# Dynamic convolution and a tanh-shrink MLP on one core: a tile in halves, a first x tile without halo, a longer accumulating DMA

## The chip, the cores and the metric

The kernel runs on one core of one Trainium2 chip. The metric is the device time of one execution in microseconds. Lower is better.

## The reference

Two steps in a row. `x` is (8, 4096, 192), `weight_gen` is (8, 4096, 8 heads, 7 taps), both f32.

```python
w = softmax(weight_gen, axis=-1)                    # 7 taps per token and head
x_pad = 6 zero rows ahead of each sequence
conv[b, s, h, g] = sum over k of w[b, s, h, k] * x_pad[b, s + k, h, g]     # 24 channels a head
h = conv.reshape(32768, 192) @ w_in                 # (192, 2048)
out = (h - tanh(h)) @ w_out                         # (2048, 192)
```

## The kernel before

**Tiling.** The 32768 tokens are cut into 32 blocks of 1024 (`NTOT`). Within a block each of the 128 partitions holds 8 neighbouring tokens (`J`), and its x tile holds 14 rows: 6 rows of halo ahead of the 8 (`HALO + J`). Partitions overlap in their halo, so that each of the 7 taps is a plain slice of the tile. The 192 channels are handled as three chunks of 64 (`NC`, `R`).

**Convolution.** `products` multiplies the x rows by the softmax weights, one instruction a tap, into bf16 tiles: `even` (taps 0, 2, 4), `odd` (taps 1, 3, 5) and `last` (tap 6). GpSimd (POOL) does nearly all of these; VectorE (DVE) does four taps of block 0 and two of block 1. From block 3 on, a DMA issued by POOL adds the first 4096 of the 4608 elements of `odd` to `even` in place (L201), so that fewer tiles have to be summed. `conv` then transposes and sums the tiles on TensorE (PE) against an identity, accumulating in PSUM: groups `even` 0 to 2, `last`, and for chunk 2 alone also the pair of `odd` that the DMA leaves out. ScalarE (ACT) copies the sum to `convT` (L244).

**MLP.** `gemm1` makes one of 16 f tiles: six matmuls into a PSUM tile `ph` of 1024 columns (L257), a tanh on ACT (L267), and a subtraction on DVE that reads the PSUM tile again and writes bf16 `gt` (L269). There are three PSUM buffers for `ph` and for the transposes' `pc`, taken in turn. `gemm2` sums one token block of the previous block's 16 `gt` tiles (L289), and ACT copies the result out (L307).

**Order.** The order of the instructions on each engine is written out by hand (`manual_schedule`). The main loop runs over blocks n; inside, eight steps p each do f tiles 2p and 2p+1 of block n and one `gemm2` of block n-1. The transposes of block n+1 come at p = 6, behind f tiles 12 and 13 and ahead of f tiles 14 and 15. The products of block n+2 are put on POOL at p = 0, so POOL works about two blocks ahead. A dependency (L177) holds their first instruction back until the last subtraction then issued.

**Start.** SyncE (SP) issues the loads of `weight_gen` and x: for block 0 the zero rows of the halo, row 0, partitions 1 to 15, partitions 16 to 127. POOL issues the load of `w_in` in two parts, f tiles 0 to 7 ahead of its products and 8 to 15 behind its products of block 0 (`FA`); each part is copied once more within SBUF, by a DMA issued from ACT and from SP (L369).

Of the kernel before, what the change touches and what calls it, by code (L numbers as in the profile page):

```python
# [11 lines left out]
ACT = mybir.ActivationFunctionType  # L12
# [4 lines left out]
def kernel(  # L17
# [8 lines left out]
    nc = tc.nc  # L26

    B, S, D = x.shape
    H, K = weight_gen.shape[2], weight_gen.shape[3]
    G = D // H  # L30
    F = moe_w_in.shape[1]
    P = nc.NUM_PARTITIONS
    R = P // 2
    HALO = K - 1

    J = 8
    TOK = P * J
# [3 lines left out]
    NTOT = B * NSB  # L41
    NFT = F // P
    NC = D // R
    GC = G // NC
    NPAIR = K // 2
    ACC = NPAIR * J * D - J * R
    PLAIN = (0, 1, 2)
    assert S % TOK == 0 and D % R == 0 and H * GC == R and F % P == 0
    assert NFT == 2 * J, "one token block of the second matmul per pair of f tiles"
# [23 lines left out]
    prods_of = {}  # L73
    conv_of = {}
    g_of = {}
    last_act = {}
    g1_act = {}
    last_sub = {}
    last_wsm = {}

    def order(inst, other, reason):
        tc.add_manual_dep(
            inst.ins,
            other.ins.name,
            mybir.DependencyInfo(mybir.DependencyClass.Sync, mybir.DependencyReason.DATA),
            reason=reason,
        )

    def load_wg(n):
        b, s = divmod(n, NSB)  # L90
        s0 = s * TOK
        wg_t = wgpool.tile([P, J, H, K], FP32, name="wg_t")
        nc.sync.dma_start(  # L93
            out=wg_t[:],
            in_=weight_gen[b, s0 : s0 + TOK].rearrange("(p j) h k -> p j h k", p=P),
        )
        wg_of[n] = wg_t

    def load_x(n):
        b, s = divmod(n, NSB)  # L100
        s0 = s * TOK

        x_t = xpool.tile([P, HALO + J, D], FP32, name="x_t")

        def rows(p0, p1):
            win = x[b, s0 + p0 * J - HALO : s0 + p0 * J - HALO + 1]
            nc.sync.dma_start(
                out=x_t[p0:p1, :, :],
                in_=bass.AP(
                    tensor=win.tensor,  # L110
                    offset=win.offset,
                    ap=[[J * D, p1 - p0], [D, HALO + J], [1, D]],
                ),
            )

        if s == 0:
            nc.sync.dma_start(  # L117
                out=x_t[0:1, 0:HALO, :],
                in_=zero[:].rearrange("o (h d) -> o h d", h=1).to_broadcast([1, HALO, D]),
            )  # L120
            nc.sync.dma_start(  # L121
                out=x_t[0:1, HALO : HALO + J, :],
                in_=x[b, 0:J].rearrange("(p j) d -> p j d", p=1),
            )

            rows(1, 16)
            rows(16, P)
        else:
            rows(0, P)
        x_of[n] = x_t  # L130
# [31 lines left out]
    def scale(eng, wsm, e_t, zr):  # L162
        return eng.tensor_mul(  # L163
            wsm.rearrange("p j h k -> p (j h) k"),
            e_t[:].rearrange("p j h k -> p (j h) k"),
            zr.rearrange("p (n o) -> p n o", o=1).to_broadcast([P, J * H, K]),
        )

    def products(n, on_vector=(), sums=None, hooks={}, behind=None):
        x_t = x_of.pop(n)  # L170
        wsm, wsm_v, e_t, zr = wsm_of.pop(n)
        if e_t is not None:
            first = scale(nc.gpsimd, wsm[:], e_t, zr[:])
            if behind is not None:


                order(first, behind, "pace")  # L177
        in_pairs = n not in PLAIN

        even = ppool.tile([P, NPAIR, NC, J, H, GC], BF16, name="even")  # L180
        odd = ppool.tile([P, NPAIR, NC, J, H, GC], BF16, name="odd")
        last = ppool.tile([P, NC, J, H, GC], BF16, name="last")
        dst = {}
        for i in range(NPAIR):
            dst[2 * i] = even[:, i]
            dst[2 * i + 1] = odd[:, i]
        dst[K - 1] = last[:]
        if -1 in hooks:
            hooks[-1]()
        for k in range(K):  # L190
            eng, w = (nc.vector, wsm_v) if k in on_vector else (nc.gpsimd, wsm[:])
            eng.tensor_mul(  # L192
                dst[k].rearrange("p c j h g -> p j h c g"),
                x_t[:, k : k + J, :].rearrange("p j (h c g) -> p j h c g", h=H, c=NC),
                w[:, :, :, k : k + 1]
                .rearrange("p j h (k o) -> p j h k o", o=1)
                .to_broadcast([P, J, H, NC, GC]),
            )
            if k == K - 2 and in_pairs:

                nc.gpsimd.dma_start(  # L201
                    out=even[:].rearrange("p i c j h g -> p (i c j h g)")[:, 0:ACC],
                    in_=odd[:].rearrange("p i c j h g -> p (i c j h g)")[:, 0:ACC],
                    accum_op=mybir.AluOpType.add,
                    max_dma_last_dim=4096,
                )
            if k in hooks:
                hooks[k]()
        if in_pairs:
            groups = [even[:, i] for i in range(NPAIR)] + [last[:]]  # L210
            prods_of[n] = [
                groups + ([odd[:, NPAIR - 1]] if c == NC - 1 else []) for c in range(NC)
            ]
        else:
            prods_of[n] = [[dst[k] for k in (sums or range(K))]] * NC

# [32 lines left out]
        if parts[-1][-1] == NC - 1:  # L249
            prods_of.pop(n)  # L250

    def gemm1(n, f):
        convT = conv_of[n]
        ph = psum_h.tile([P, 2, HT], FP32, name="ph", tag="ph")
        for c in range(NC):
            for r in range(2):
                nc.tensor.matmul(  # L257
                    ph[:, r, :],
                    lhsT=w_in[r * R : (r + 1) * R, c, f * P : (f + 1) * P],
                    rhs=convT[r * R : (r + 1) * R, c, :],  # L260
                    start=(c == 0),
                    stop=(c == NC - 1),
                )
        th = tpool.tile([P, TOK], FP32, name="th")
        ph_f = ph[:].rearrange("p r t -> p (r t)")
        g1_act[0] = last_act.get(0)
        last_act[0] = nc.scalar.activation(out=th[:], in_=ph_f, func=ACT.Tanh)  # L267
        gt = gpool.tile([P, TOK], BF16, name=f"gt{f}", tag=f"gt{f}")
        last_sub[0] = nc.vector.tensor_sub(gt[:], ph_f, th[:])  # L269
        g_of.setdefault(n, []).append(gt)  # L270

    LAST = (NTOT - 1) * J
# [76 lines left out]
    def load_w_out():  # L349
        nc.gpsimd.dma_start(out=w_out[:], in_=moe_w_out.rearrange("(c p) e -> p c e", c=NFT))  # L350

    FA = 8 * P

    def load_w_in(f0, f1):

        for c in range(NC):
            src = moe_w_in[c * GC : c * GC + 1, f0:f1]
            dma = nc.gpsimd.dma_start(
                out=w_in[0:R, c, f0:f1],
                in_=bass.AP(  # L360
                    tensor=src.tensor, offset=src.offset, ap=[[G * F, H], [F, GC], [1, f1 - f0]]
                ),
            )
            if f0 == 0:

                order(dma, last_wsm[0], "order of the loads")

    def copy_w_in(f0, f1, eng):
        eng.dma_start(out=w_in[R:P, :, f0:f1], in_=w_in[0:R, :, f0:f1])  # L369

    def rest_of_w_in():
        load_w_in(FA, F)

    load_wg(0)
    load_x(0)
    softmax_exp(0)
    softmax_norm(0, obank[0])
    load_wg(1)
    load_x(1)
    load_w_in(0, FA)  # L380
    products(
        0,
        on_vector=(3, 4, 5, 6),
        sums=(3, 0, 4, 5, 1, 6, 2),
        hooks={2: rest_of_w_in},
    )
    softmax_exp(1)
# [1 line left out]
    load_wg(2)  # L389
    copy_w_in(0, FA, nc.scalar)  # L390
    copy_w_in(FA, F, nc.sync)
    products(1, on_vector=(0, 1), hooks={4: load_w_out})
    conv(0, (0, 1), (2,))
    load_x(2)
    for n in range(NTOT):
        if n + 3 < NTOT:
            load_wg(n + 3)
            load_x(n + 3)
        for p in range(J):
            gemm1(n, 2 * p)  # L400
            gemm1(n, 2 * p + 1)
            if n == 0 and p == 1:
                softmax_exp(2)
            if p == 5 and n + 3 < NTOT:
                softmax_exp(n + 3)
            if n >= 1:
                gemm2((n - 1) * J + p)
            if p == 0 and 1 <= n < NTOT - 2:
                products(n + 2, behind=last_sub[0] if n > 1 else None)
            if n + 1 < NTOT:  # L410
                if p == (6 if n > 0 else 7):
                    conv(n + 1, (0, 1))
                if p == (6 if n > 1 else 7):
                    conv(n + 1, (2,))
            if n == 0 and p == 2:
                softmax_norm(2)
                products(2)
            if p == 6 and n + 3 < NTOT:
                softmax_norm(n + 3)
# [33 lines left out]
```

The softmax here doesn't subtract the row's maximum and nothing guards it: scores larger than these inputs give would overflow.

## Time and profile before

| What | Value |
|---|---|
| Median of 3 runs | 770.32 us (770.04 to 771.87) |
| The profiled execution | 770.86 us, span 768.7 us |
| PE, PEld busy | 736.7 us (96%), 583.1 us (76%) |
| DVE, ACT, POOL busy | 652.9 us, 640.8 us, 695.2 us |
| L269, subtraction, 512 times | 1219 ns each |
| L267, tanh, 512 times | 1022 ns each |
| L192 on POOL, one tap | 2903 ns each |
| L201, accumulating DMA, 29 times | 1202 ns to issue, 8.8 us to landing |

The profile is of one execution. PE is TensorE's matmuls and PEld its weight loads, which overlap. A line of the timeline has the start and the duration in microseconds, the engine, the line of the kernel, the operation, what it writes and reads, how many instructions are merged, and in brackets the idle time before it and what ended that. A line that gives three numbers behind a count has the shortest, median and longest duration in nanoseconds, and the first and last start.

### The profile page before, as it was taken

The page shows a single profiled execution, that of the slowest core. Times are in us where ns is not written, and L with a number is a line of the kernel's source. Part 1 is how long each engine was busy: PE and PEld are TensorE (multiplying, and loading weights), DVE is VectorE, ACT ScalarE, POOL GpSimd, SP SyncE. Part 2 cuts the span into 40 slices and gives each one's busy share as a digit, 9 for nine tenths or more (in the row PEclk, how much of TensorE's full clock was granted, in tenths as well). Part 3 has the DMA queues.
Part 4 walks back from the last instruction along what each step waited for, and adds up shares of the span by engine and source line. Part 5 has one row for each costly group of instructions (what it writes and reads, how often), then busy time and mean ns, then how long its engine had stood idle before and what let it go on. Part 6 is the DMA issues. An engine that isn't in the chain of part 4 may idle for free.

```text
span 768.7 us, 32330 instructions
## 1 busy us (share of the span) xinstructions
PE 736.7 (96%) x14784; PEld 583.1 (76%) x14784; DVE 652.9 (85%) x595; ACT 640.8 (83%) x865; POOL 695.2 (90%) x290
## 2 busy tenths in 40 slices
PE   2799999999999999999999999999999999999997
PEld 2377787777777777788777777777778777787777
DVE  5987888888898888889888888888888988888883
ACT  1777878888888888888888888888888888888883
POOL 5999999999999999999999999999999999999100
PEclk9999999999999999999999999999999999999999
DMA  7823776555677555577655557765556765542412
GB/s 209 184 81 87 182 181 150 118 145 147 169 182 174 131 129 148 150 180 182 164 123 133 150 160 182 180 128 137 143 150 172 182 181 115 125 142 72 98 43 84
DMA packets 25847, 111.37 MB, mean 145 GB/s; under 512 B 4800, under 2 KB 9456, under 8 KB 21624
## 3 DMA queue, kind: packets, MB, share of 16 engines
q1 hardware_dynamic: 14688, 76.95, 29.9%
q0 software_dynamic: 10816, 31.99, 25.8%
q8 instruction: 115, 1.88, 1.0%
q10 hardware_dynamic: 208, 0.39, 0.2%
q14 instruction: 20, 0.16, 0.1%
HBM read 54.49 MB, written 25.17 MB: 104 GB/s over the span
## 4 chain that ended last, share of the span: by engine, by line
PE 93%; DVE 2%; issue 1%; POOL 1%; DMA 1%; ACT 1%; SPq 0%; POOLq 0%
PE ph L257 43%; PE obank L289 43%; PE pc L233 6%; DVE gt L269 2%; PE po L323 1%; DMA x_t<-in_x_dram 1%; POOL even L192 1%; ACT th L267 0%; ACT convT L244 0%; POOL odd L192 0%; DVE zr L151 0%; DVE zsum L145 0%; SPq L117 0%; SPq L93 0%; SPq L121 0%
## 5 line engine op out<-in xcount | busy, mean ns | idle before, releaser
L269 DVE TENSOR_TENSOR gt<-ph,th 128x1024 bf16<-128x1024 f32 x512 | 602.8, 1219 | 93.3 <-ACT th L267 92.7
L267 ACT ACTIVATE th<-ph 128x1024 f32<-128x1024 f32 x512 | 497.2, 1022 | 65.7 <-PE ph L257 64.9
L257 PE MATMUL ph<-convT,w_in 64*128 64x512 bf16 x3072 | 382.1, 378 | 7.5 <-DVE gt L269 5.0
L289 PEld LDWEIGHTS <-gt 64*128 64x128 bf16 x7936 | 345.1, 94 | 53.4 <-issue 2.5
L289 PE MATMUL obank<-w_out,gt 64*128 64x192 bf16 x7936 | 374.6, 243 | 2.9 <-issue 2.1
L192 POOL TENSOR_TENSOR even<-x_t,wsm 128x1536 bf16<-128x1536 f32 x94 | 272.8, 2903 | 3.9 <-DMA x_t<-in_x_dram 1.6
L192 POOL TENSOR_TENSOR odd<-x_t,wsm 128x1536 bf16<-128x1536 f32 x93 | 269.9, 2903 | 0.0
L257 PEld LDWEIGHTS <-w_in 64*128 64x128 bf16 x3072 | 180.1, 94 | 108.4 <-issue 11.8
L192 POOL TENSOR_TENSOR last<-x_t,wsm 128x1536 bf16<-128x1536 f32 x31 | 103.4, 3336 | 0.0
L307 ACT ACTIVATE out_sb<-obank 128x192 f32<-128x192 f32 x248 | 81.9, 330 | 10.5 <-PE obank L289 4.6
L244 ACT ACTIVATE convT<-pc 128x1024 bf16<-128x1024 f32 x64 | 48.9, 808 | 31.6 <-PE pc L233 31.5
L233 PE MATMUL pc<-ident,even 64*128 64x64 bf16 x2304 | 47.9, 192 | 2.9 <-POOL even L192 1.5
L233 PEld LDWEIGHTS <-even 64*128 64x128 bf16 x2304 | 42.7, 96 | 4.1 <-issue 2.2
L201 POOL DMA_DIRECT2D even<-odd x29 | 34.9, 1205 | 9.1 <-POOL odd L192 9.1
L163 POOL TENSOR_TENSOR wsm<-e_t,zr 128x448 f32<-128x448 f32 x30 | 41.7, 1390 | 0.0
L233 PE MATMUL pc<-ident,odd 64*128 64x64 bf16 x448 | 15.5, 198 | 13.1 <-DVE odd L192 12.8
L135 ACT ACTIVATE e_t<-wg_t 128x448 f32<-128x448 f32 x32 | 18.5, 578 | 8.2 <-DMA wg_t<-in_weight_gen_dram 8.2
L233 PE MATMUL pc<-ident,last 64*128 64x64 bf16 x768 | 23.3, 192 | 1.8 <-issue 1.7
L145 DVE TENSOR_REDUCE zsum<-e_t 128x64 f32<-128x448 f32 x32 | 19.5, 609 | 2.9 <-ACT e_t L135 2.9
L233 PEld LDWEIGHTS <-odd 64*128 64x128 bf16 x448 | 11.3, 100 | 13.6 <-DVE odd L192 12.9
L151 DVE RECIPROCAL zr<-zsum 128x64 f32<-128x64 f32 x30 | 16.6, 553 | 3.0
L233 PEld LDWEIGHTS <-last 64*128 64x128 bf16 x768 | 17.0, 96 | 2.2 <-issue 1.8
(20 smaller groups left out, 48.7 us busy)
## 6 DMA issues: line engine op xcount, KB each, us to landing
x_t<-in_x_dram SPq DMA_DIRECT2D x24, 1344.0 KB
even<-odd POOLq DMA_DIRECT2D x29, 1024.0 KB, 8.8
out_dram<-out_sb SPq DMA_DIRECT2D x31, 768.0 KB
x_t<-in_x_dram SPq DMA_DIRECT2D x8, 1176.0 KB
wg_t<-in_weight_gen_dram SPq DMA_DIRECT2D x32, 224.0 KB
x_t<-in_x_dram SPq DMA_DIRECT2D x8, 157.5 KB
w_in<-in_moe_w_in_dram POOLq DMA_DIRECT2D x6, 128.0 KB, 7.5
w_out<-in_moe_w_out_dram POOLq DMA_DIRECT2D x1, 768.0 KB, 10.8
```

The source lines that it names most:

```text
L135: nc.scalar.activation(out=e_t[:].rearrange("p j h k -> p (j h k)"), in_=wg_t[:].rearrange("p j h k -> p (j h k)"), func=ACT.Exp,)
L145: nc.vector.reduce_sum(out=zsum[:], in_=e_t[:].rearrange("p j h k -> p (j h) k"), axis=AX.X)
L163: return eng.tensor_mul(wsm.rearrange("p j h k -> p (j h) k"), e_t[:].rearrange("p j h k -> p (j h) k"), zr.rearrange("p (n o) -> p n o", ...
L192: eng.tensor_mul(dst[k].rearrange("p c j h g -> p j h c g"), x_t[:, k : k + J, :].rearrange("p j (h c g) -> p j h c g", h=H, c=NC), w[:, : ...
L201: nc.gpsimd.dma_start(out=even[:].rearrange("p i c j h g -> p (i c j h g)")[:, 0:ACC], in_=odd[:].rearrange("p i c j h g -> p (i c j h g)" ...
L233: nc.tensor.matmul(pc[:, r, col : col + R], lhsT=prods[c][gi][r * R : (r + 1) * R, c, 2 * j : 2 * j + 2].rearrange("p j h g -> p (j h g)") ...
L244: nc.scalar.activation(out=convT[:, c0 : c0 + nch, :].rearrange("p c (j r t) -> p r (c j) t", r=2, t=R), in_=pc[:, :, 0 : nch * JH * R].re ...
L257: nc.tensor.matmul(ph[:, r, :], lhsT=w_in[r * R : (r + 1) * R, c, f * P : (f + 1) * P], rhs=convT[r * R : (r + 1) * R, c, :], start=(c == ...
L267: last_act[0] = nc.scalar.activation(out=th[:], in_=ph_f, func=ACT.Tanh)
L269: last_sub[0] = nc.vector.tensor_sub(gt[:], ph_f, th[:])
L289: mm = nc.tensor.matmul(po[:, 0:D], lhsT=g_of[n][f][r * R : (r + 1) * R, col : col + P], rhs=w_out[r * R : (r + 1) * R, f, :], start=(r == ...
L307: last_act[0] = nc.scalar.activation(out=out_sb[:, j, :], in_=po[:, 0:D], func=ACT.Copy)
```

## The change

Three edits. (1) In blocks 1 to 30, f tile 12, the one at p = 6, does its tanh and its subtraction in two halves of 512 columns. (2) The accumulating DMA covers all three pairs in full, 4608 elements a partition, given as three rows of 1536; the transposes of the last `odd` pair for chunk 2 go. (3) Block 0: x comes as 8 rows for all partitions first, then the halo of partitions 16 to 127, that of 1 to 15, and the zero rows last; the taps are taken in the order 6, 0, 3, 1, 4, 5, 2 and summed in the order 6, 3, 0, 4, 5, 1, 2; the first part of `w_in` has 7 f tiles instead of 8.

```diff
-    ACC = NPAIR * J * D - J * R
...
-        if s == 0:
-            nc.sync.dma_start(out=x_t[0:1, 0:HALO, :], in_=zero...)
-            nc.sync.dma_start(out=x_t[0:1, HALO : HALO + J, :], in_=x[b, 0:J]...)
-            rows(1, 16)
-            rows(16, P)
+        if n == 0:
+            rows(0, P, HALO, HALO + J)
+            rows(16, P, 0, HALO)
+            rows(1, 16, 0, HALO)
+            no_halo()
+        elif s == 0:
+            no_halo()
+            rows(0, 1, HALO, HALO + J)
             rows(1, 16)
             rows(16, P)
...
-        for k in range(K):
+        for k in order_of or range(K):
...
                 nc.gpsimd.dma_start(
-                    out=even[:].rearrange("p i c j h g -> p (i c j h g)")[:, 0:ACC],
-                    in_=odd[:].rearrange("p i c j h g -> p (i c j h g)")[:, 0:ACC],
+                    out=even[:].rearrange("p i c j h g -> p i (c j h g)"),
+                    in_=odd[:].rearrange("p i c j h g -> p i (c j h g)"),
                     accum_op=mybir.AluOpType.add,
                     max_dma_last_dim=4096,
                 )
...
-            groups = [even[:, i] for i in range(NPAIR)] + [last[:]]
-            prods_of[n] = [
-                groups + ([odd[:, NPAIR - 1]] if c == NC - 1 else []) for c in range(NC)
-            ]
+            prods_of[n] = [[even[:, i] for i in range(NPAIR)] + [last[:]]] * NC
...
-    def gemm1(n, f):
+    def gemm1(n, f, parts=1):
...
-        last_act[0] = nc.scalar.activation(out=th[:], in_=ph_f, func=ACT.Tanh)
-        last_sub[0] = nc.vector.tensor_sub(gt[:], ph_f, th[:])
+        for q in range(parts):
+            t0, t1 = q * TOK // parts, (q + 1) * TOK // parts
+            last_act[0] = nc.scalar.activation(
+                out=th[:, t0:t1], in_=ph_f[:, t0:t1], func=ACT.Tanh
+            )
+            last_sub[0] = nc.vector.tensor_sub(gt[:, t0:t1], ph_f[:, t0:t1], th[:, t0:t1])
...
-    FA = 8 * P
+    FA = 7 * P
...
-        on_vector=(3, 4, 5, 6),
-        sums=(3, 0, 4, 5, 1, 6, 2),
+        on_vector=(6, 3, 4, 5),
+        order_of=(6, 0, 3, 1, 4, 5, 2),
+        sums=(6, 3, 0, 4, 5, 1, 2),
...
-            gemm1(n, 2 * p)
+            gemm1(n, 2 * p, 2 if p == 6 and 0 < n < NTOT - 1 else 1)
```

More of the change, by code (lines that the diff above doesn't have):

```diff
@@ L103, in load_x, with rows @@
         x_t = xpool.tile([P, HALO + J, D], FP32, name="x_t")
-        def rows(p0, p1):
-            win = x[b, s0 + p0 * J - HALO : s0 + p0 * J - HALO + 1]
+        def rows(p0, p1, r0=0, r1=HALO + J):
+            win = x[b, s0 + p0 * J - HALO + r0 : s0 + p0 * J - HALO + r0 + 1]
             nc.sync.dma_start(
-                out=x_t[p0:p1, :, :],
+                out=x_t[p0:p1, r0:r1, :],
                 in_=bass.AP(
@@ L111, in rows, with no_halo @@
                     offset=win.offset,
-                    ap=[[J * D, p1 - p0], [D, HALO + J], [1, D]],
+                    ap=[[J * D, p1 - p0], [D, r1 - r0], [1, D]],
                 ),
             )
-        if s == 0:
+        def no_halo():
             nc.sync.dma_start(
@@ L120, in load_x @@
             )
[L121 to L124, printed above, removed]
+        if n == 0:
[6 more added lines that the diff above has]
+            rows(0, 1, HALO, HALO + J)
             rows(1, 16)
@@ L167, in scale, with products @@
         )
-    def products(n, on_vector=(), sums=None, hooks={}, behind=None):
+    def products(n, on_vector=(), order_of=None, sums=None, hooks={}, behind=None):
         x_t = x_of.pop(n)
@@ L360, in load_w_in @@
                 in_=bass.AP(
-                    tensor=src.tensor, offset=src.offset, ap=[[G * F, H], [F, GC], [1, f1 - f0]]
+                    tensor=src.tensor,
+                    offset=src.offset,
+                    ap=[[G * F, H], [F, GC], [1, f1 - f0]],
                 ),
```

## The prediction, made before the changed kernel was run

> **What bounds the kernel now.** I read the page's busy shares and chain first, then the timeline of one late block, then the issues on GpSimd, then the start.
>
> ```profile
> PE 736.7 (96%) x14784; PEld 583.1 (76%) x14784; DVE 652.9 (85%) x595; ACT 640.8 (83%) x865; POOL 695.2 (90%) x290
> ...
> PE 93%; DVE 2%; issue 1%; POOL 1%; DMA 1%; ACT 1%; SPq 0%; POOLq 0%
> ```
>
> TensorE carries the chain. POOL's 90% needs care: it is idle only at the two ends, so in between it is full too. The timeline around the transposes of block 25 (the other late blocks repeat it every 22.63 us):
>
> ```profile
> 589.56 1.94 ACT L267 ACTIVATE th<-ph 128x1024 f32<-128x1024 f32 x2
> ...
> 590.61 2.36 DVE L269 TENSOR_TENSOR gt<-ph,th 128x1024 bf16<-128x1024 f32 x2 [0.26 <-ACT th L267]
> ...
> 592.46 1.51 ACT L244 ACTIVATE convT<-pc 128x1024 bf16<-128x1024 f32 x2 [0.60 <-PE pc L233]
> ...
> 592.68 0.20 PEld L233 LDWEIGHTS <-odd 64*128 64x128 bf16 x8
> ...
> 592.80 1.20 PEld L257 LDWEIGHTS <-w_in 64*128 64x128 bf16 x12
> ...
> 593.02 1.47 PE L257 MATMUL ph<-convT,w_in 64*128 64x512 bf16 x12
> ...
> 593.88 1.94 ACT L267 ACTIVATE th<-ph 128x1024 f32<-128x1024 f32 x2
> ...
> 594.94 2.36 DVE L269 TENSOR_TENSOR gt<-ph,th 128x1024 bf16<-128x1024 f32 x2 [0.79 <-ACT th L267]
> ...
> 595.63 1.48 PE L257 MATMUL ph<-convT,w_in 64*128 64x512 bf16 x12
> ```
>
> The reader is to see a small stall that the page doesn't list. Tile 14's weights load at 592.80; in other pairs the matmul follows 0.08 later (588.61 and 588.69, 595.55 and 595.63). Here it starts at 593.02, 0.05 after the subtraction of tile 13 ends (590.61 + 2.36 = 592.97): three `ph` buffers, and tile 14 takes that of tile 13. So TensorE loses 592.88 to 593.02, 0.14 us a block. The eight `odd` transposes (592.68 to 592.80) lie ahead of this wait.
>
> ```profile
> 573.94 1.20 POOL L201 DMA_DIRECT2D even<-odd  x1 [0.30 <-POOL odd L192]
> 574.72 3.37 POOL L192 TENSOR_TENSOR last<-x_t,wsm 128x1536 bf16<-128x1536 f32 x1
> 577.59 1.42 POOL L163 TENSOR_TENSOR wsm<-e_t,zr 128x448 f32<-128x448 f32 x1
> ...
> 596.59 1.20 POOL L201 DMA_DIRECT2D even<-odd  x1 [0.30 <-POOL odd L192]
> ```
>
> POOL's own period is 596.59 - 573.94 = 22.65 us: as long as TensorE's, with no wait but that ahead of the DMA. What saves it is a lead. The last accumulating DMA is issued at 710.17, lands 8.8 us later in the median (11.1 at most), and its transposes start at 727.09; the first is issued at 75.77 for 88.47. Landing leaves about 4 us at the start, 6 to 8 later.
>
> **What the Trainium skill says.** "DMA: Bandwidth & Descriptors", Anatomy of one DMA, has many descriptors emitted before their incremental cost shows. The trace agrees:
>
> ```profile
> L201 POOL DMA_DIRECT2D even<-odd x29: 1202/1202/1244, 75.8 to 710.2; - x29
> L350 POOL DMA_DIRECT2D w_out<-in_moe_w_out_dram x1: 1233/1233/1233, 29.2 to 29.2; - x1
> L358 POOL DMA_DIRECT2D w_in<-in_moe_w_in_dram x6: 562/580/788, 6.8 to 20.0; - x6
> ```
>
> POOL's queue moves 2064 packets in the stretch of `w_out` and 272 in that of one accumulation, and both issues cost 1.2 us; `w_in` with 64 rows costs 0.58. The issue goes with rows (9.4 ns each), not pieces. The same page, SDMA does more than copy, caps an accumulating element at 2048 elements; 272 packets are 128 rows in two pieces of 2048 and 16 for the semaphore, so it agrees. Three pieces of 1536 a row then make 384. "GPSIMD Engine Reference", section 4, has a pair of cores write the descriptors; `last`, starting 0.78 after the DMA and taking 3.37 instead of 2.90, fits. "VectorE: DVE Perf Modes", the TRN2 errata, charges a fixed latency per instruction; here 192 elements take 357 ns, 1024 take 1219, 1536 take 1748: 1.036 ns an element and 158 ns fixed.
>
> **Part 1, the tile in halves (blocks 1 to 30).** One tanh and one subtraction become two each: 30 more on ACT, 30 more on DVE. ACT: 192 elements 330 ns, 1024 1022 ns, so 0.832 ns an element and 0.60 us for 512 (the 512-wide copy at L244 takes 0.60). Start to start, 1024 take 0.92 (1.94 - 1.02), so 512 take 0.92 - 0.43 = 0.49. DVE start to start: 1.14, so 512 take 0.61. In the block above, the first half's tanh ends at 590.16, tile 13's tanh starts at 589.56 + 2 x 0.49 = 590.55 instead of 590.48 and ends at 591.57. DVE is free at 590.28 (588.00 + 2 x 1.14), does the halves at 590.29 and 590.90, and tile 13 at 591.60 (0.03 after its tanh) instead of 591.755; it ends at 592.81. Tile 14 may start at 592.86, **0.16 earlier**. Behind the later tanh wait the `out_sb` copy (0.07 later, into ACT's 0.60 of idle) and the copies to `convT`, which wait for TensorE. Nothing there becomes late.
>
> What is late next: tile 14's tanh. ACT's `convT` copies start at 592.46, set by transposes that the change leaves alone, and occupy it to 593.38 + 0.48 = 593.86; the tanh gains 0.02 only. Its subtraction then ends at about 596.14, and the next block's second tile, which takes that buffer, can start at 596.19. It now starts at 595.63 + 0.65 (half of 594.31 - 593.02) = 596.28. **Gain: 0.09 us a block**. Below: 0, should another wait sit there; above: 0.16, should that one not bind. I take 0.09 x 29 = **2.6 us** (0 to 4.6).
>
> **Part 2, all 4608 elements.** Removes 8 matmuls and 8 loads a block, 15 ns each, 0.12 us; this lies ahead of the same wait, so alone it is worth nothing, and with part 1 TensorE is ready at 592.76, before the 592.86 of the gate. I count 0. It adds an eighth to the bytes and half to the pieces. Landing: by bytes 6.4 us of transfer (16 packets an engine of 0.4) become 7.2, so 9.6 us; by pieces 9.6, so 12 us. Both stay inside the 4 us. Packets of other queues have to share: PE's short gaps put to "issue" (5.7 us in all) could move either way by 1 us. The issue: 0 if rows count (taken), +0.41 us if a descriptor costs what lies between `w_in` (64: 0.58) and the accumulation (256: 1.20), 3.2 ns; +0.60 at 4.7 ns each. Behind it on POOL stand `last`, the next `wsm` and all later products.
>
> **Part 3, the start.**
>
> ```profile
> 10.32 2.90 POOL L192 TENSOR_TENSOR even<-x_t,wsm 128x1536 bf16<-128x1536 f32 x1 [1.57 <-DMA x_t<-in_x_dram]
> ...
> 20.73 4.85 PE L257 MATMUL ph<-convT,w_in 64*128 64x512 bf16 x24 [0.91 <-ACT convT L244]
> 20.85 3.39 PEld L257 LDWEIGHTS <-w_in 64*128 64x128 bf16 x18 [1.14 <-DMA w_in<-w_in]
> ```
>
> Two paths meet at 20.8: POOL's three products after x, and the copy of `w_in`. SP issued the large x load at 2.86, behind the zero rows (1.19) and two small loads; now it goes at 1.19, the halo at 1.6 and 2.0, the zeros last at 2.4; the next `wg` and x stay at 3.3 and 3.8. Bytes are equal. The stream cannot overtake that of `wg`, whose reader starts at 3.38, so I give it not 1.7 us but 0.7: x lands that much earlier and POOL (busy issuing until 8.76) starts at 9.6 instead of 10.32. DVE does tap 6 before the halo lands, but POOL's three products end last. On the other path, 7 tiles instead of 8 take an eighth off the load and the copy (issued at 17.11, 3.7 us): about 0.5. First tile: 0.6 earlier. Tiles 0 to 15 of block 0 then run on DVE without a gap (7.21 us for 6), so this reaches the end. The price: tile 7 now needs the second part, whose copy SP issues at 26.33; with the first copy's 3.7 us it is there at 30.1. It moves 0.6 earlier and has 9/8 of the bytes: about 30. Tile 7 wants it at 29.53 - 0.6 = 28.9, but DVE's softmax work at 30.53 gives it until about 30.2: just covered; uncovered it costs up to 0.8. **Gain 0.6** (-0.8 to 1.2).
>
> **Sum.** 2.6 + 0.6 = 3.2. The profiled execution took 770.86 (span 768.7), so 767.7; the median of the runs, 770.32, is 0.5 below its own, so **767.2 us**. A difference under 0.3% (2.3 us) can't be told from none.
>
> **Rivals.** (a) *Nothing to be seen*, 768.0 to 772.6: the wait moves from tile 14 to the next block's second tile at once (0 for part 1), or the start loses what it wins. For it: the margin there is 0.09 of 22.63. About 770. (b) *POOL becomes the bound*: the descriptor price per piece. The last landing, 710.17 + 10.4 = 720.6, moves to 720.6 + 0.8 - 0.6 + 28e, and the last transposes would like to start at 727.1 - 3.2 = 723.9: gains shrink from e = 0.11 us, and from 0.31 the kernel is slower. With 0.41, +5.2, **775.5 us**; with 0.60, +10.5, 780.8. For it: POOL is full for 670 us. Against it: `w_out`. (c) *The change doesn't do what it says*: the two contiguous dimensions are joined and cut in another way; the bytes are the same, so the time falls under the forecast or under (b).
>
> **Chances.** Forecast 0.5; (a) 0.3; (b) 0.2. Range 765.0 (both gains near their upper ends) to 774.5, which leaves out most of (b).
>
> **What would show it.** Right: L201 at 1.20, tile 14 0.05 behind a subtraction ending 0.16 earlier relative to the transposes, block period 22.54, 384 + 16 packets, first POOL product near 9.6. Wrong: L201 over 1.3 us and transposes waiting for a landing; a period still at 22.63; tile 7 waiting for `w_in` beyond 30.2.

## The result and the profile after

The change made the kernel slower: 791.11 us in the median of 4 runs (789.72 to 792.73) against 770.49 us for the kernel before beside it, a ratio of 1.0265 with an interval of 1.0238 to 1.0292. The profiled execution took 792.73 us with a span of 791.0; before it was 770.86 and 768.7. So 22.3 us of span have to be found.

The busy shares and the chain of the page after, to be held against those of before:

```profile
PE 738.9 (93%) x14552; PEld 580.8 (73%) x14552; DVE 657.4 (83%) x625; ACT 641.5 (81%) x895; POOL 698.8 (88%) x290
...
PE 71%; DVE 16%; ACT 8%; issue 3%; POOL 1%; DMA 1%; SPq 0%; POOLq 0%
```

All engines do nearly the same work as before (VectorE 657.4 us against 652.9, ScalarE 641.5 against 640.8), in a longer span. What changed is the chain: TensorE carried 93% of it and now carries 71%; VectorE has 16% and ScalarE 8%. Work of those two that used to lie beside TensorE now lies in its way, again and again. The waits, with the engine and line that waits, what it waits for, the sum in us, how often, and the longest:

```profile
ACT th L272 <- DVE gt L275: 24.8, 30, 0.8
POOL wsm L167 <- DVE gt L275: 13.8, 22, 0.7
```

The first line has no counterpart before: 30 times, once for each halved tile, a tanh waits 0.83 us for a subtraction. The timeline of block 25 after, around the same place that the prediction showed (start, duration, and in brackets the idle time ahead and what ended it):

```profile
604.72 2.95 DVE L275 TENSOR_TENSOR gt<-ph,th 128x1024 bf16<-128x1024 f32 x3 [0.26 <-ACT th L272]
...
606.28 0.60 ACT L272 ACTIVATE th<-ph 128x512 f32<-128x512 f32 x1
...
607.71 1.51 ACT L272 ACTIVATE th<-ph 128x512 f32<-128x512 f32 x2 [0.83 <-DVE gt L275]
...
608.03 0.88 PE L234 MATMUL pc<-ident,even 64*128 64x64 bf16 x48
608.33 0.69 DVE L275 TENSOR_TENSOR gt<-ph,th 128x512 bf16<-128x512 f32 x1 [0.66 <-ACT th L272]
...
609.25 1.23 DVE L275 TENSOR_TENSOR gt<-ph,th 128x1024 bf16<-128x1024 f32 x1 [0.22 <-ACT th L272]
...
610.53 1.47 PE L258 MATMUL ph<-convT,w_in 64*128 64x512 bf16 x12 [0.81 <-DVE gt L275]
```

The reader is to follow it downwards. The first half's tanh ends at 606.88. The second half's could start there; it starts at 607.71, when the first half's subtraction, the last of the three in the first line, has ended (604.72 + 2.95 = 607.67). Tile 13's tanh is pushed behind it, tile 13's subtraction starts at 609.25 and ends at 610.47, and tile 14, whose `ph` buffer that subtraction frees, starts 0.05 later at 610.53. From the first transposes to tile 14's first matmul pass 610.53 - 608.03 = 2.50 us; before, the trace has 1.71. The difference, 0.79, is the whole change of the block period: 23.42 us after, 22.63 before. The block period is the time from one block's transposes to the next one's, and conv(n) stands for the start of those of block n. Over the 28 blocks between conv(3) and conv(31) that is 22.1 us of the 22.66 that this stretch grew (661.28 against 638.62); the start is 1.2 us earlier and the end, with one more halved tile, 0.9 us longer. The halves alone explain the sum; they do not show yet whether the other two parts were free.

The accumulating DMA after, and POOL's first product:

```profile
L205 POOL DMA_DIRECT2D even<-odd x29: 1281/1291/1323, 74.8 to 729.7; - x29
```

```profile
9.31 2.90 POOL L196 TENSOR_TENSOR even<-x_t,wsm 128x1536 bf16<-128x1536 f32 x1 [0.60 <-DMA x_t<-zero]
```

The issue takes 1.29 us instead of 1.20 and lands after 10.3 us in the median (9.0 to 11.4), instead of 8.8. The first two of them now land 1.1 and 0.9 us ahead of their transposes, where before it was 3.9 and 4.0, and POOL itself waits once for one, 3.3 us. One accumulation is 384 packets and 16 for the semaphore. The first product starts at 9.31 instead of 10.32.

### The profile page after: what moved, and what is told of

Read it like the earlier page. It is cut to its first block, busy times and chain, and to the rows that moved or that the text cites. A ratio compares the mean times of both kernels' runs of the same rounds, so it can differ in the third digit from the quotient of the medians.

```text
span 791.0 us, 31925 instructions
## 1 busy us (share of the span) xinstructions
PE 738.9 (93%) x14552; PEld 580.8 (73%) x14552; DVE 657.4 (83%) x625; ACT 641.5 (81%) x895; POOL 698.8 (88%) x290
## 3 DMA queue, kind: packets, MB, share of 16 engines
q8 instruction: 114, 1.87, 1.0%
## 4 chain that ended last, share of the span: by engine, by line
PE 71%; DVE 16%; ACT 8%; issue 3%; POOL 1%; DMA 1%; SPq 0%; POOLq 0%
PE ph L258 36%; PE obank L295 33%; DVE gt L275 16%; ACT th L272 7%; PE po L329 1%; DMA x_t<-zero 1%; POOL even L196 1%; PE pc L234 1%; POOL odd L196 0%; ACT convT L245 0%; SPq L106 0%; DVE zr L155 0%; DVE zsum L149 0%; SPq L92 0%; DVE out_sb L341 0%
## 5 line engine op out<-in xcount | busy, mean ns | idle before, releaser
L275 DVE TENSOR_TENSOR gt<-ph,th 128x1024 bf16<-128x1024 f32 (+1 forms) x542 | 607.3, 1160 | 113.4 <-ACT th L272 113.3
L272 ACT ACTIVATE th<-ph 128x1024 f32<-128x1024 f32 (+1 forms) x542 | 502.4, 975 | 106.6 <-PE ph L258 81.0
L295 PEld LDWEIGHTS <-gt 64*128 64x128 bf16 x7936 | 346.8, 94 | 53.0 <-issue 2.6
L258 PEld LDWEIGHTS <-w_in 64*128 64x128 bf16 x3072 | 178.1, 94 | 133.0 <-issue 37.6
L313 ACT ACTIVATE out_sb<-obank 128x192 f32<-128x192 f32 x248 | 82.3, 332 | 10.3 <-PE obank L295 5.9
L245 ACT ACTIVATE convT<-pc 128x1024 bf16<-128x1024 f32 x64 | 49.4, 832 | 13.8 <-PE pc L234 13.7
L234 PE MATMUL pc<-ident,even 64*128 64x64 bf16 x2304 | 48.0, 192 | 6.3 <-issue 3.2
L234 PEld LDWEIGHTS <-even 64*128 64x128 bf16 x2304 | 44.8, 96 | 8.8 <-issue 4.5
L205 POOL DMA_DIRECT2D even<-odd x29 | 37.4, 1289 | 9.0 <-POOL odd L196 9.0
L167 POOL TENSOR_TENSOR wsm<-e_t,zr 128x448 f32<-128x448 f32 x30 | 31.6, 1055 | 13.8 <-DVE gt L275 13.8
L234 PE MATMUL pc<-ident,last 64*128 64x64 bf16 x768 | 23.2, 192 | 8.3 <-DVE last L196 8.3
L234 PEld LDWEIGHTS <-last 64*128 64x128 bf16 x768 | 17.1, 96 | 8.3 <-DVE last L196 8.3
L329 PE MATMUL po<-w_out,gt 64*128 64x192 bf16 x256 | 11.0, 243 | 0.0
L329 PEld LDWEIGHTS <-gt 64*128 64x128 bf16 x256 | 10.8, 93 | 0.0
## 6 DMA issues: line engine op xcount, KB each, us to landing
even<-odd POOLq DMA_DIRECT2D x29, 1152.0 KB, 10.3
```

Of the source, the lines that this page charges most:

```text
L167: return eng.tensor_mul(wsm.rearrange("p j h k -> p (j h) k"), e_t[:].rearrange("p j h k -> p (j h) k"), zr.rearrange("p (n o) -> p n o", ...
L205: nc.gpsimd.dma_start(out=even[:].rearrange("p i c j h g -> p i (c j h g)"), in_=odd[:].rearrange("p i c j h g -> p i (c j h g)"), accum_o ...
L234: nc.tensor.matmul(pc[:, r, col : col + R], lhsT=prods[c][gi][r * R : (r + 1) * R, c, 2 * j : 2 * j + 2].rearrange("p j h g -> p (j h g)") ...
L245: nc.scalar.activation(out=convT[:, c0 : c0 + nch, :].rearrange("p c (j r t) -> p r (c j) t", r=2, t=R), in_=pc[:, :, 0 : nch * JH * R].re ...
L258: nc.tensor.matmul(ph[:, r, :], lhsT=w_in[r * R : (r + 1) * R, c, f * P : (f + 1) * P], rhs=convT[r * R : (r + 1) * R, c, :], start=(c == ...
L272: last_act[0] = nc.scalar.activation(out=th[:, t0:t1], in_=ph_f[:, t0:t1], func=ACT.Tanh)
```

## The experiments

Two theories stood. **W**: the wait of the second tanh is the cause. **D**: the longer DMA is the cause, directly or by what queues behind it. It turned out that the first holds for most of the loss and that the second comes back for the rest. The runs fall into three groups, each on a chip of its own beside the kernel before: e1 to e4 (770.03 us for the kernel before), e5 to e8 (770.26) and e9 to e12 (770.51). Ratios are to the kernel before of the same group.

**e1, the change without the halves.**

```
-            gemm1(n, 2 * p, 2 if p == 6 and 0 < n < NTOT - 1 else 1)
+            gemm1(n, 2 * p)
```

> The changed kernel with tile 12 whole again; the full accumulating DMA and the new start stay. Theory W (the second half's tanh has to wait for the first half's subtraction, and that wait is the whole loss): the period of a block falls from 23.42 us to 22.63 and the time to about 769.5 (770.5 less the 1.0 by which the first f tile of block 0 starts earlier). Rival D (the longer accumulating DMA, 10.3 us to landing instead of 8.8, fills GpSimd and the DMA engines): most of the loss stays, 785 to 791.

Measured: 774.95 us (773.74 to 775.62), ratio 1.0058 (1.0045 to 1.0072). Neither end: taking the halves out wins 16 us of the 21, and the other two parts together are not free but cost 4.9 us.

**e2, the halves alone on the kernel before.**

> The kernel before with tile 12 in halves, nothing else. Theory W: 0.78 us in each of some 29 blocks, 770.5 + 22.6 = about 793, the period 23.4 and the second tanh starting 0.03 us behind the first half's subtraction. Rival D: 768 to 771, since the DMA is the old one.

Measured: 789.81 us, ratio 1.0256 (1.0242 to 1.0270), 3 us under what W had, with the expected period of 23.42 us. The halves make the longer period by themselves.

**e3, both tanhs ahead of both subtractions**, in an otherwise unchanged kernel after:

```
-        for q in range(parts):
-            t0, t1 = q * TOK // parts, (q + 1) * TOK // parts
+        cuts = [(q * TOK // parts, (q + 1) * TOK // parts) for q in range(parts)]
+        for t0, t1 in cuts:
             last_act[0] = nc.scalar.activation(
...
+        for t0, t1 in cuts:
             last_sub[0] = nc.vector.tensor_sub(gt[:, t0:t1], ph_f[:, t0:t1], th[:, t0:t1])
```

> The changed kernel with both tanhs of tile 12 written ahead of both subtractions. The program then has no wait between the two tanhs; instead the first subtraction waits for the second tanh. Theory W: tile 13's subtraction ends about 0.15 us later than with a whole tile (the second tanh ends 0.07 later, the split costs the subtraction 0.07), so the period is 22.7 to 22.8 and the time 771 to 774. Rival (any split is as bad, by its fixed costs or by its place): 785 to 791.

Measured: 775.03 us, ratio 1.0066 (1.0053 to 1.0079), 1 us above the expected range and the same as with a whole tile (e1). The long wait is gone, but not its kind: now the first subtraction waits for the second tanh. Ahead of conv(27) the first tanh ends at 638.51, the second at 639.00, and the first subtraction starts at 639.03. The period is 22.76 us.

**e4, the same as the kernel after, with the dependency of the second tanh on the first subtraction declared away:**

```
+        prev = None
...
+            if prev is not None:
+                tc.declare_no_dep(last_act[0].ins, prev.ins, reason="other PSUM bank")
+            prev = last_sub[0] = nc.vector.tensor_sub(gt[:, t0:t1], ph_f[:, t0:t1], th[:, t0:t1])
```

This is no race: the two halves share only the PSUM tile `ph`, which both engines read, and they lie in different banks. The Trainium skill's "PSUM — Partial Sum Buffer", section "PSUM bank collisions raise a hardware error", has two engines in the same bank and quadrant (32 partitions) at once end in an error, two reads too, and lets different banks run clean; under "Specifications (TRN2)" the same page gives a bank as 512 float32 values, and each half is 512. The trace agrees that the two may run together: ahead of conv(27) the second tanh runs from 638.27 to 638.87 and the first subtraction from 638.49 to 639.17.

> The changed kernel with the wait of the second tanh for the first subtraction declared needless: the two read different PSUM banks[...]. Nothing else differs. Theory W with the prediction's own working: tile 13's subtraction ends 0.16 us earlier than with a whole tile, the next wait catches it 0.09 us later in the block, period 22.54, time about 767. Rival (the gain is eaten at once by another wait): as with the whole tile, 769 to 770.

Measured: 773.28 us, ratio 1.0047 (1.0034 to 1.0059). The wait is gone and the period is 22.54, as W had it; the time is 6 us above what W had, as what e1 lost is still in it. The timeline of e4 at block 28:

```profile
659.90 3.68 DVE L278 TENSOR_TENSOR gt<-ph,th 128x1024 bf16<-128x1024 f32 x4
...
660.32 2.00 ACT L273 ACTIVATE th<-ph 128x512 f32<-128x512 f32 x3
...
662.07 0.88 PE L234 MATMUL pc<-ident,even 64*128 64x64 bf16 x48
...
663.64 1.27 PE L258 MATMUL ph<-convT,w_in 64*128 64x512 bf16 x10
```

Three tanhs and four subtractions run as one group each, with no bracket: nobody waits. From transposes to tile 14 are 1.57 us.

**e12, a buffer of its own for the second half's tanh**:

```
+            th_q = th if q == 0 else tpool.tile([P, TOK], FP32, name="th2", tag="th2")
```

> The kernel after, with a buffer of its own for the second half of tanh(tile 12); two reads of the same PSUM tile remain. If the wait comes from the buffer of tanh, it goes: 773 us, as without the wait. If it comes from the two engines' reads of the PSUM tile, all stays as in the kernel after: 789 to 793 us, with the second tanh behind the first subtraction.

Measured: 790.15 us, ratio 1.0257 (1.0243 to 1.0271), with the wait as in the kernel after:

```profile
ACT th L273 <- DVE gt L276: 24.9, 30, 0.8
```

So the wait does not hang on the tanh buffer. What the second tanh and the first subtraction still have in common is the PSUM tile that both read, and e4 shows that it is a dependency of the program that holds the tanh, since declaring it away ends the wait. So the framework makes the second reader wait for the first, for the whole tile. W stands. What it doesn't explain is e1's 4.9 us.

**Where e1's time goes.** The waits of TensorE's weight loads show it, before and then e1 (L233 of before is L234 of e1, the transposes; "issue" is a pause for which the profile shows no releaser):

```profile
PEld L233 <- issue: 4.4, 7, 1.8
```

```profile
PEld L234 <- issue: 10.0, 11, 2.5
```

One of the eleven, in block 6 of e1:

```profile
160.69 0.10 PEld L234 LDWEIGHTS <-even 64*128 64x128 bf16 x2
...
162.33 0.38 PEld L234 LDWEIGHTS <-even 64*128 64x128 bf16 x22 [1.54 <-issue]
```

TensorE stops for 1.54 us in the middle of a run of transposes, all of whose inputs are there. Counted from the trace's first TensorE instruction, a load and its matmul as two and semaphore instructions with them, the first instruction after such a pause has number 194 modulo 256 in all nine pauses that e1 has after the start (blocks 4 to 26, even blocks only; the other two belong to block 1), and 193 or 194 in the kernel before. (The expectations below count from another start and call the place row 69.) The page's queue "instruction" moves 114 packets, 1.87 MB, so 16384 bytes a packet, and TensorE has some 29,100 instructions in the program of e1: one packet for 256 of them. In the trace these nine pauses end 1.2 to 1.5 us after such a packet has ended. **Theory F** was that TensorE runs out of instructions in the transposes, where it consumes them fastest (15 ns a load and a matmul): with 96 transposes a block has 897 TensorE instructions, 3.5 packets and one, so every second block has the boundary at nearly the same place; with 104 it has 913 and the boundary wanders. D says that the longer DMA is to blame. The next two kernels have one each without the other.

**e5, short DMA, 96 transposes; e6, long DMA, 104 transposes.** In e5 the sum lacks a part and in e6 it has one twice, as the expectations say. **e11, the new start alone**, is the fourth corner. Tile 12 is whole in all three.

> The kernel after with tile 12 whole, and with the old, shorter accumulating DMA (4096 of the 4608 elements), but still only 96 transposes a block: the last odd pair of chunk 2 is left out of the sum, so this part of the computation is missing. Theory F (TensorE waits for its instructions: a block of 897 TensorE rows puts the boundary of a 256-row packet into the same place of the transposes of every second block): the stalls stay, at row 69 of 256 of the program, so 774 to 776 us like the kernel with the long DMA. Theory D (the longer DMA, 10.3 us instead of 8.8, holds up the packets or the transposes): the stalls go, 768 to 770 us.

> The kernel after with tile 12 whole and the long accumulating DMA, but with 104 transposes a block again: the last odd pair of chunk 2 is added a second time by TensorE, so its sum counts it twice. F: a block has 913 TensorE rows again, the boundary wanders through the block as in the kernel before, few stalls: 768 to 770 us (770.0 less the 1.0 to 1.6 us of the start). D: the DMA is as long as in the kernel after, 774 to 776 us.

> Only the new start, with the short DMA and 104 transposes of the kernel before, tile 12 whole: the fourth corner beside 96 transposes alone (770.2), long DMA alone (771.45) and both (774.95). Start gain of 1.0 to 1.6 us alone: 768.4 to 769.0 us. The 96 transposes then cost 1.5, the long DMA 2.7, both 6.2 us: more than the sum, as FD has it. If it is at 766 us, the two costs simply add up.

"Pauses" is the time by which the stretch from conv(3) to conv(31) is longer than 28 periods (22.63 each), from one trace of each kernel; "minus before" is against the kernel before of the same group:

```
                             us      ratio (interval)             minus before    pauses, us
before                                                                               5.0
e11  short DMA, 104        768.90   0.9980 (0.9973 to 0.9988)        -1.6             4.8
e5   short DMA, 96         770.21   0.9995 (0.9987 to 1.0003)         0.0             6.1
e6   long DMA, 104         771.45   1.0014 (1.0007 to 1.0020)        +1.2             7.3
e1   long DMA, 96          774.95   1.0058 (1.0045 to 1.0072)        +4.9            11.0
```

The start is worth 1.6 us. From there 96 transposes alone cost 1.6, the long DMA alone 2.8, and both 6.5: more than their sum by 2.2 us (0.8 to 3.7, an estimate from the four intervals), and the pauses follow. So neither F nor D alone: e5 came out just above D's range and e6 between the two, nearer to F's. In e5 the pauses lie at number 193 or 194 too, up to block 14, and then they stop, although the boundary is still there. The windows ahead of conv(20) tell the two apart; a line has the stretch, its length, the busy time and the instructions of PE, PEld, DVE, ACT and POOL, the granted clock, and in the last two columns the share of the DMA engines that are busy and GB/s. e1, from 3 us ahead of the transposes to their start:

```profile
477.94:478.94 1.00, 1.00 (x20) 0.74 (x16) 1.00 (x2) 1.00 (x3) 1.00 (x1) 1.00 0.97 406
478.94:479.94 1.00, 1.00 (x16) 0.69 (x15) 1.00 (x1) 1.00 (x3) 1.00 (x1) 1.00 0.93 371
479.94:480.94 1.00, 1.00 (x30) 1.00 (x27) 0.74 (x2) 1.00 (x2) 1.00 (x2) 1.00 0.18 58
```

and e5:

```profile
474.63:475.63 1.00, 1.00 (x20) 0.74 (x17) 1.00 (x2) 1.00 (x3) 1.00 (x1) 1.00 0.52 193
475.63:476.63 1.00, 1.00 (x16) 0.69 (x15) 1.00 (x1) 1.00 (x3) 1.00 (x1) 1.00 0.05 20
476.63:477.63 1.00, 1.00 (x30) 1.00 (x26) 0.74 (x2) 1.00 (x2) 1.00 (x2) 1.00 0.00 0
```

The boundary is at load 59 of the transposes in both. In e1 the DMA engines are full until 1 us ahead; the packet of instructions starts 0.88 us ahead of the transposes, and TensorE pauses 0.47 us. In e5 they are free about 1.5 us earlier, the packet starts 2.04 us ahead, and there is no pause. What fills them is a train: the accumulating DMA from 8 us after a conv, then x for a later block and the output. In e1 ahead of conv(20) x is issued 9.9 us after the conv before, while the accumulation fills the engines, and its packets move only from 14.7 us on, when that has drained. A longer accumulation pushes the end of the train up to the next conv. **Theory FD**: a packet of instructions behind the train comes late, and where its boundary lies in the transposes TensorE notices.

The packets can be set against the boundaries one by one, since each trace has as many of the one as of the other (114 in e1). A packet starts as TensorE crosses a boundary and brings what is wanted at the next. Where the DMA engines are under a tenth busy around the crossing, it starts 0.4 us behind it in the median; where they are over nine tenths busy, 3.5 us (670 and 628 crossings in the 14 kernels of this document). No boundary in any of them is crossed less than 0.98 us after the packet for it has ended, and of the 79 pauses over 0.2 us in their transposes from block 2 on, 77 lie at a boundary and end 0.98 to 1.64 us after the packet. Ahead of conv(20) in e1 the boundary before is crossed at 477.25, the packet starts at 479.98 and ends at 480.92, and TensorE goes on at 482.31. It had run out at 481.84: 256 instructions that end in transposes took it 4.6 us, where those of the matrix products alone take 7.7.

**e7, the version that F and D would both build**: halves without the wait, new start, short DMA, 104 transposes.

> The version that both theories would build: halves of tile 12 without the wait of the second tanh, first x tile in its new order, the short DMA and 104 transposes of the kernel before. If start, halves and stalls add up: 770.0 less 1.3 (start) less 1.7 to 2.6 (halves) gives 766 to 767 us. If the stalls depend on something else than the 96 transposes or the long DMA, 771 to 773 us, as the same kernel with both.

Measured: 768.03 us, ratio 0.9966 (0.9954 to 0.9979), 1 us above the expected range. Its pauses are 6.1 us above 28 periods of 22.54: the train ends where it did, so part of the halves' 2.5 us was given back.

**e8, the boundary moved by 64 instructions**: e1 with, ahead of all else, 32 times

```
+        nc.tensor.matmul(obank[1][0:R, 0:R], lhsT=ident[0:R, 0:R], rhs=ident[0:R, 0:R], start=True, stop=True)
```

> The kernel after with tile 12 whole, and 32 small matmuls (a weight load and a multiplication each, 64 TensorE rows, on the identity) ahead of the first block; their output isn't used. They move every later TensorE instruction by 64 rows against the packets and cost under 1 us while TensorE has nothing else to do. F: the stalls leave loads 54 to 67 of the transposes, where they all were; row 69 of 256 now lies at loads 24 to 35 of the even blocks, and from about block 10 on at loads 87 to 95 of the odd ones. In the kernel before those places cost 0 to 0.45 us, so 769 to 773 us. D, or any cause by time or place in the block: the stalls stay at loads 54 to 67, 774 to 776 us.

Measured: 772.93 us, ratio 1.0031 (1.0021 to 1.0041). The pauses moved as computed: of those over 0.2 us, blocks 4 and 6 have them at loads 35 and 34, blocks 21, 23 and 25 at 90, 89 and 88, none at 54 to 67, and the time above 28 periods fell from 11.0 to 4.7 us. Counted with the 64 new instructions, they still have number 193 or 194. Block 2's transposes, which had none, took one of 3.62 us, so the total gained only 2. F's forecast came true, and D's, that they stay at 54 to 67, did not: the place in the program counts.

**e9, x later.** The kernel is e1, with the load of x for block n + 3 issued behind the copies of conv(n + 1), when the DMA engines are empty:

```
-            load_x(n + 3)
+            if n < 2:
+                load_x(n + 3)
...
                 if p == (6 if n > 1 else 7):
                     conv(n + 1, (2,))
+                if p == 6 and 2 <= n and n + 3 < NTOT:
+                    load_x(n + 3, conv_act[0])
```

`load_x` puts `order(dma, behind, "later")` on its first piece, and `conv_act[0]` is the last copy to `convT`. In the blocks that begin a sequence the load of row 0 now also comes ahead of the zero rows, so that the first piece carries this order.

> The kernel after with tile 12 whole (long DMA, 96 transposes), and from block 2 on the load of x for block n + 3 is issued behind the copies of conv(n + 1), some 11 us later than now. In the runs so far the DMA engines are full from 8 us after a conv to 1 or 2 us ahead of the next (the accumulating DMA, then x and the output), and empty from then on; the long DMA pushes that tail up to the conv. Theory FD (the packet of TensorE's instructions waits behind the tail of the load of x, and the row of the packet's boundary decides whether TensorE notices): without the tail the fetch starts earlier and the stalls go, 768 to 770 us (start gain of 1.3 alone gives 768.7). Theory F alone (the place of the boundary is enough): the stalls stay, 774 to 776 us. If the later x holds up POOL: over 776 us.

Measured: 767.48 us, ratio 0.9960 (0.9946 to 0.9974): just under FD's range and 7.5 us less than e1, with the same DMA, the same transposes and the boundary where it was. The waits of its weight loads, whose transposes are at L239:

```profile
PEld L239 <- issue: 5.3, 13, 0.7
```

The longest pause fell from 2.5 to 0.7 us, and the time above 28 periods from 11.0 to 3.5. They didn't go entirely: the products and with them the accumulating DMA come later now, so it is this DMA that runs until 1.5 us ahead of the conv, and a packet can still meet it.

**e10, e7 with the later x**, with which the shorter accumulation ends 3 to 4 us ahead of the conv.

> The fastest version so far (halves without the wait, new start, short DMA, 104 transposes: 768.0 us) with the later load of x. FD: its stalls (about 6 us above the period of 22.54 in blocks 3 to 31) shrink to 1 or 2 us, 763 to 765 us. F alone: 768 us as before.

Measured: **761.96 us** (761.76 to 762.21), ratio 0.9890 (0.9877 to 0.9904), the fastest of all and 1 us under FD's range. Its chain, and its waits at the transposes (L243):

```profile
PE 94%; DVE 2%; POOL 1%; issue 1%; ACT 1%; DMA 0%
```

```profile
PEld L243 <- issue: 1.3, 3, 0.6
```

From conv(3) to conv(31) it takes 631.71 us, 0.6 more than 28 periods of 22.54, and from block 3 on no pause in the transposes is over 0.2 us. The sum closes: start 1.6, halves 28 x 0.09 = 2.5, pauses 5.0 - 0.6 = 4.4, together 8.5; the median fell by 770.51 - 761.96 = 8.55. It is good to some tenths, as 0.2 of the start's 1.6 are pauses too (5.0 and 4.8 in the table).

What is shown is that the pauses lie at fixed numbers of the program, move with it, and shrink with the train that precedes them; that a packet is called for as TensorE crosses a boundary; and that it starts late where the engines are full. That it waits in the same DMA engines behind other packets fits this, but the trace doesn't name the engine of a packet. e9 also moves POOL's products and the accumulation, so it is the times of the packets, and not e9 alone, that tie the gain to the train. The kernel after fits from the other side: with its period of 23.42 us the DMA engines are empty from 2 us ahead of conv(26) on, and after block 6 its transposes show no pause over 0.2 us. Its stretch is 5.6 us longer than 28 of its own periods, where e1's is 11.0 longer, so the halves (19.8 in e2) and the rest (4.9 in e1) add up to only 20.6.

## Why the prediction was wrong, by its steps

**What bounds the kernel** was right. TensorE sets the pace, tile 14 waits for tile 13's subtraction, and 0.05 us after a subtraction it starts, before (592.97 and 593.02) and after (610.47 and 610.53).

**Part 1** failed in one step: "tile 13's tanh starts at 589.56 + 2 x 0.49". It let the second half's tanh follow the first at once, 0.49 us behind its start. It costed instructions and what each engine is busy with, and put at nothing, without a reason, the order between two engines that read one PSUM tile. That wait was not in the trace of before, where a tile's tanh and subtraction are one pair and follow each other anyway, so the trace could not price it, and the bounds (0 to 4.6 us of gain) excluded a loss without a reason for it. The wait takes 0.83 us, and tile 14 came 0.79 later instead of 0.16 earlier. The rest of the step was right: without the wait (e4) the period is the predicted 22.54, and the gate named as next, the next block's second tile 0.05 behind tile 14's subtraction, is where it was put (0.053). Of the gain of 2.6 us little reached the total: e4 is 1.7 us under e1 by the medians and 0.8 by the ratios, whose intervals overlap, and e7 is 0.6 to 1.1 under e11. The period fell as forecast, but the pauses took some back (e7 has 6.1 us of them, e11 4.8).

**Part 2** was counted at 0 with ±1 us for the pauses. Its two checks held: the issue grew by 0.09 us, not the 0.41 or 0.60 of a price by piece, and the landing (10.3 us, nearer the 9.6 by bytes than the 12 by pieces) stayed inside the lead, if only by 0.9 us at its least. The mis-sized term is "PE's short gaps put to issue ... could move either way by 1 us": with the other parts as in e1 they grew by 6.2 us over e11. The prediction looked for the DMA's cost at its reader; it lay with the traffic behind it, and taking out the 8 transposes was not free either (1.6 us, e5 against e11), since with 897 instructions a block the boundary stays at one place of the transposes.

**Part 3** was right in direction, and low: 1.6 us by e11's median, beyond the stated 1.2, which e11's interval (0.9 to 2.1 us) does not exclude. POOL's first product came at 9.31 (9.6 forecast), the first tile at 19.71 instead of 20.73, 1.0 earlier where 0.6 was forecast. Tile 7 was not held up.

**The rivals.** (a) needed a gain to vanish; a loss came. (b) named POOL as the mechanism on the slow side: POOL still waits for its pace 22 times after (13.8 us above), so it wasn't the bound. Its break-even was also set too high: with its own numbers, (727.1 - 720.8) / 28, the kernel is slower from 0.22 us of issue on, and 0.31 is where that passes 2.3 us. (c) is out: 384 packets, 96 transposes, halves of 512. No case named a wait between ScalarE and VectorE, so 791 lay beyond every one.

## What to carry to other kernels

Before a tile is cut so that two engines may overlap on it, ask what orders their accesses: here the framework ordered two reads of one PSUM tile although the halves lie in two banks, and the cut cost 0.79 us a block until that order was taken away. When a transfer grows, follow what is queued behind it as well as its reader: here loads of x, and behind them TensorE's own instructions. And where a dense run of small instructions pauses for "issue", count instructions modulo 256 and see how full the DMA engines are just ahead: here, moving a load into their idle stretch gave 6 us (e10 against e7) and 7.5 us (e9 against e1).

## What the hardware showed that was not expected

- TensorE can run dry of instructions: pauses of 0.2 to 3.6 us in transposes at 15 ns a pair, 77 of 79 from block 2 on at number 193 or 194 modulo 256 of its program, ending 1.0 to 1.6 us after a 16384-byte packet.
- The packet starts about when TensorE crosses the boundary before, 0.4 us behind it in the median with nearly empty DMA engines and 3.5 us with full ones, so that other transfers of the same core have a part in whether TensorE stops.
- An addition of 64 instructions at the start moved and changed such pauses (e8), so a kernel's time can move by some us through edits that change only how many instructions come ahead.
- The issue of the accumulating DMA grew by 0.09 us for half as many pieces again, and its landing by 0.9 us (e1) to 1.5 us (the kernel after) for an eighth more bytes.
